# The last 64 features of q and k as one 128-column group in two token halves, q/k weights issued from ScalarE's queue, and a new operation order, in a fused attention and MLP kernel

## Chip, core and metric

The kernel runs on one core of one Trainium2 chip, as one program. The metric is device microseconds of one execution. All times are from the profile page, from the trace or from the timed runs.

## What is computed

Input `x` is 2048 tokens by 448 features in bf16. Two blocks follow each other, each behind a layer norm of its own and each added to its input:

```python
def _A_ref(x, wqkv, wo):                      # D = 448, H = 16 heads, Dh = 28
    W, dil = 8, 2
    qkv = (x @ wqkv).reshape(B, S, 3, H, Dh)...
    idx = pos[:, None] - arange(W)[None, :] * dil     # 8 keys, 2 tokens apart
    logits = einsum("bhsd,bhswd->bhsw", q, kg) * Dh ** -0.5
    attn = softmax(where(idx >= 0, logits, -1e9))
    o = einsum("bhsw,bhswd->bhsd", attn, vg)
    return o.reshape(B, S, D) @ wo

def _B_ref(x, w1, w2, w3, w4):                # F = 1792
    h = gelu(layernorm(x) @ w1)
    # four groups of 112 features, shifted by +1, -1, +2, -2 tokens
    hs = concatenate([g0, g1, g2, g3]) @ w2
    x1 = x + hs
    return x1 + gelu(layernorm(x1) @ w3) @ w4

h  = x + _A_ref(layernorm(x), wqkv, wo)
h2 = h + _B_ref(layernorm(h), w1, w2, w3, w4)
```

## The kernel before

The tokens are worked on in four blocks of 512 (t = 0 to 3) for attention and the first part of the MLP, and in five units of 2, 4, 4, 4 and 2 tiles of 128 tokens for the rest. A phase has a letter and the number of its block: N1 (norm), A1 (transpose, then q and k), V (values), A2 (products of q with the eight shifted keys, and their sums over heads), S (softmax), A3 (attention times values), O (output projection), B1 and M (second norm, `w1`, gelu), B2 and T (`w2`, third norm), W3 (`w3`, gelu), B3 (`w4`, store).

The program records all operations first (`_Sched.group`, reached through `mms`, `steps`, `act`, `dve`, `pool` and `dma`), each with what it depends on. `ORDER` is a list of operation numbers: `_Sched.arrange` gives each engine its operations in that order, hands out the buffers (eight PSUM banks, `actT`, `lntm` and others) in that order, and derives the waits. Every engine's queue and SyncE's DMA queue (SP) is therefore a fixed list. `OTHER` names the operations that go to a second engine that could also do them. Since all instructions are emitted by one line, the profile gives the line L1010 for nearly all of them; they are told apart by tile names.

The contraction over 448 features is cut into chunks at 0, 128, 192 and 320, so that each matmul uses 64 rows: `duo` runs two sums side by side, one on partitions 0 to 63 and one on 64 to 127, and swaps them for the second half, which waits for the first (`sdeps`). A pair of such matmuls is written "64*128" in the profile: 64 rows, 128 columns of the array.

Features 0 to 383 of q and of k are three groups of 128 columns each. The last 64 features of q and of k are a fourth group (the lines from `X, Y = _Tile(P_bank), _Tile(P_bank)` on in `phase_A1`). There the array is cut into 64 by 64 pieces ("64*64" in the profile), 28 matmuls for each block of tokens. Even pieces of 64 tokens land on partitions 0 to 63 and odd ones on 64 to 127. Then `X` (q) is copied to `qT` with one copy, `Y` (k) to `kr` with one copy, and two or three small copies fill the 16 columns ahead of each piece of `kr`, from which the shifted keys of A2 are read.

At the start `WARM` matmuls of 512 columns on the identity keep TensorE busy (`keep_busy`); `FILL` can put more between the first transposes. SP issues all loads: tiles 0, 1, and 2 with 3 of `x`, the q/k weights in two halves (`load_rows`, "arena<-in_A_wqkv_dram", 448 KB each), tiles 4 to 7, the v weights, the rest. Every matmul of q and k needs both halves of the q/k weights.

Of the kernel before, what the change touches and what calls it, by code (L numbers as in the profile page):

```python
# [50 lines left out]
"""  # L51
OTHER = """
92 182 483 489 492 495 546 552
"""
FULL = (4,)
FILL = (0, 0, 0, 0)
WARM = 11
FIRST = ((0, 1), (1, 1), (2, 2))


class _Pool:


# [219 lines left out]
def bass_sequential_preLN__sliding_local_dilated__mixer_s_mlp__prompt_kernel(  # L283
# [9 lines left out]
    PADK = 16  # L293
# [20 lines left out]
    with ExitStack() as es:  # L314
# [60 lines left out]
        def shifted(t, c):  # L375
            return bass.AP(AR, A_KV + t * KVB + c * KVW + PADK, [[A_END, 128], [64, 8] if c < 3 else [KW, 4], [-DIL, NW], [1, 64]])
# [675 lines left out]
```

## Time and profile before

| | |
|---|---|
| median of three timed runs | 189.51 us (188.73 to 191.31) |
| span of the profiled execution, first to last instruction | 186.4 us |
| time of the profiled execution | not on its page; the median lies 3.1 us above the span |
| TensorE matmul (PE) busy | 180.3 us, 97% of the span, 2496 matmuls |
| TensorE weight load (PEld) busy | 94.0 us, 50% |
| VectorE (DVE) busy | 127.0 us, 68%, 225 instructions |
| ScalarE (ACT) busy | 122.1 us, 65%, 289 instructions |
| GpSimd (POOL) busy | 24.0 us, 13%, 59 instructions |
| DMA | 18.59 MB, 41.5% of 16 engines' span on the program's queue |

A row of the timeline has the start, the time from the first start to the last end, engine, line, operation, the tiles written and read, rows and columns of the array for TensorE, shape and count; in brackets the idle time before and what ended it. A row of groups has the busy time, the mean ns of one, and the idle time before.

### The profile page before, as it was taken

To read this page: it belongs to the slowest core of one execution; us is meant where nothing else is said; L and a number is where in the kernel's file an instruction comes from. 1 tells how busy PE (TensorE), PEld (TensorE's weight loads), DVE (VectorE), ACT (ScalarE), POOL (GpSimd) and SP (SyncE) were. 2 spreads that over 40 slices of the span, in tenths; PEclk is the share of its full clock that TensorE was granted. 3 is DMA by queue.
4 is the path that set the end of the run, shared out by engine and by line. 5 is a ranking of instruction groups with operands and counts; after the bars stand their busy time and mean duration, and the time that the engine had idled before them with its cause. 6 is when DMAs were issued, how large, how long until landed. Compare 5 with 4: busy or idle time off the path is not lost.

```text
span 186.4 us, 5772 instructions
## 1 busy us (share of the span) xinstructions
PE 180.3 (97%) x2496; PEld 94.0 (50%) x2496; DVE 127.0 (68%) x225; ACT 122.1 (65%) x289; POOL 24.0 (13%) x59
## 2 busy tenths in 40 slices
PE   6899998999999999999999999999999999999994
PEld 2474333445544565765455544554445544555663
DVE  6799999999999999999476587614087274000403
ACT  3549999898999999957959489503833004730340
POOL 4320000000000000425300000170002805000000
PEclk9999999999999999999999999999999999999999
DMA  5999025865515667914360201491111602300121
GB/s 134 356 282 182 16 51 130 198 216 71 144 38 110 115 216 165 307 53 45 73 116 10 58 8 26 88 141 54 29 40 41 116 0 52 106 0 4 49 98 49
DMA packets 33633, 18.59 MB, mean 100 GB/s; under 512 B 21208, under 2 KB 33096, under 8 KB 33608
## 3 DMA queue, kind: packets, MB, share of 16 engines
q1 hardware_dynamic: 33608, 18.23, 41.5%
q8 instruction: 19, 0.31, 0.6%
q14 instruction: 6, 0.05, 0.1%
HBM read 8.14 MB, written 1.84 MB: 54 GB/s over the span
## 4 chain that ended last, share of the span: by engine, by line
PE 79%; DVE 14%; ACT 4%; DMA 1%; issue 0%; SPq 0%
PE ps L1010 79%; DVE qk_r L1010 9%; DVE st L1010 1%; ACT lntm L1010 1%; DMA xin<-in_A_x_dram 1%; DVE lntm L1010 1%; ACT L1010 1%; DVE mx L1010 1%; DVE xin L1010 1%; ACT arena L1010 1%; ACT h3T L1010 1%; DVE pb L1010 0%; DVE ls L1010 0%; DVE mv L1010 0%; ACT rs_x L1010 0%
## 5 line engine op out<-in xcount | busy, mean ns | idle before, releaser
L1010 PE MATMUL ps<-actT,arena 64*128 64x512 bf16 (+2 forms) x812 | 69.8, 326 | 0.9 <-DMA actT<-lntm 0.5
L1010 ACT ACTIVATE h3T<-ps 128x512 bf16<-128x512 f32 (+1 forms) x70 | 30.9, 517 | 38.5 <-PE ps L1010 38.4
L1010 PEld LDWEIGHTS ps<-actT,arena 64*128 64x128 bf16 (+1 forms) x812 | 35.4, 96 | 31.9 <-PE ps L1010 1.9
L1010 PE MATMUL ps<-arena,h3T 64*128 64x448 bf16 (+3 forms) x434 | 44.9, 343 | 0.2
L1010 ACT ACTIVATE arena<-ps 128x512 bf16<-128x512 f32 (+6 forms) x66 | 30.7, 508 | 8.5 <-PE ps L1010 8.1
L1010 PEld LDWEIGHTS ps<-arena,h3T 64*128 64x128 bf16 (+1 forms) x434 | 22.6, 94 | 20.0 <-ACT h3T L1010 0.6
L1010 DVE TENSOR_TENSOR qk_r<-arena 128x4096 bf16<-128x4096 bf16 (+1 forms) x16 | 31.9, 2013 | 0.1
L1010 DVE SCALAR_TENSOR_TENSOR qk_r<-ps,mrs,arena 128x448 bf16<-128x448 f32 (+2 forms) x17 | 10.4, 651 | 30.9 <-PE ps L1010 30.9
L1010 POOL TENSOR_TENSOR arena<-arena,xin 128x448 f32<-128x448 f32 x16 | 16.1, 1035 | 77.9 <-ACT lntm L1010 65.5
L1010 DVE TENSOR_TENSOR bd_r<-arena,bmask 80x2048 bf16<-80x2048 bf16 x16 | 19.0, 1214 | 1.7 <-PE ps L1010 1.7
L1010 DVE SCALAR_TENSOR_TENSOR arena<-xin,rs_y,ps 128x448 f32<-128x448 bf16 x16 | 10.3, 671 | 11.0 <-PE ps L1010 11.0
L1010 PE MATMUL ps<-wo_s,actT 64*128 64x448 bf16 x128 | 14.5, 350 | 0.1
L1010 PE MATMUL ps<-actT,w_s 64*112 64x512 bf16 x112 | 13.4, 379 | 0.0
L1010 PE MATMUL ps<-w_s,arena 64*128 64x448 bf16 x83 | 12.8, 349 | 0.1
L1010 PE MATMUL ps<-arena,actT 64*128 64x448 bf16 x112 | 12.3, 351 | 0.2
L1010 ACT ACTIVATE actT<-ps 128x512 bf16<-128x512 f32 (+2 forms) x19 | 11.7, 639 | 1.1 <-PE ps L1010 1.0
L1010 ACT ACTIVATE lntm<-xin,nm 128x448 bf16<-128x448 bf16 x16 | 10.6, 672 | 1.1 <-DVE nm L1010 1.1
L1010 DVE BATCH_NORM_STATS2 st<-xin 128x6 f32<-128x448 bf16 x16 | 9.2, 614 | 1.0 <-DMA xin<-in_A_x_dram 0.9
L1010 PEld LDWEIGHTS ps<-actT,w_s 64*112 64x112 bf16 x112 | 7.2, 126 | 4.4 <-ACT arena L1010 0.3
L1010 ACT ACTIVATE rs_x<-mv,epsilon 128x4 f32<-128x4 f32 (+2 forms) x16 | 4.6, 298 | 6.4 <-DVE mv L1010 6.3
L1010 PEld LDWEIGHTS ps<-w_s,arena 64*128 64x128 bf16 x83 | 5.5, 95 | 6.1 <-PE ps L1010 0.5
L1010 ACT ACTIVATE vt<-ps 128x448 bf16<-128x448 f32 x16 | 8.3, 546 | 0.5 <-PE ps L1010 0.5
(73 smaller groups left out, 161.6 us busy)
## 6 DMA issues: line engine op xcount, KB each, us to landing
arena<-in_B_w_dram SPq DMA_DIRECT2D x2, 896.0 KB, 5.9
out_dram<-qk_r SPq DMA_DIRECT2D x15, 112.0 KB, 1.8
arena<-in_B_w_dram SPq DMA_DIRECT2D x2, 784.0 KB, 7.3
vw<-vt SPq DMA_DIRECT2D x4, 320.0 KB, 4.3
vw<-vt SPq DMA_DIRECT2D x4, 256.0 KB, 4.1
arena<-in_A_wqkv_dram SPq DMA_DIRECT2D x2, 448.0 KB, 4.7
xin<-in_A_x_dram SPq DMA_DIRECT2D x2, 448.0 KB, 7.5
xin<-in_A_x_dram SPq DMA_DIRECT2D x3, 224.0 KB, 5.5
```

The costliest lines, as they stand in the source:

```text
L1010: inst = getattr(eng, meth)(**kw)
```

## The change

1. In `phase_A1` the last 64 features of q and of k become one group of 128 columns. Their weights are first copied side by side into a new tile `wl` (`setup_last`, one copy on GpSimd behind the q/k weights' arrival). The 512 tokens are two halves of 256, which are the two sums of one `duo`: 14 matmuls of 64 rows, 128 columns and 256 tokens. Of each half, partitions 0 to 63 of the bank hold q and 64 to 127 hold k. Two copies go to `qT`, two to `kr`, one small copy fills the columns ahead of the second half and, but for the last block, one those of the next block.
2. `kr` is now one row of 16 + 256 columns for each half. `phase_A2`, the end of S and `phase_A3` address tokens in the new arrangement, with the same shapes of work.
3. Both halves of the q/k weights are issued by ScalarE. The load of tiles 4 and 5 now waits for the landing of tiles 2 and 3.
4. `ORDER` and `OTHER` are new, `WARM` goes from 11 to 7, and one filler matmul stands between the first transposes.

```diff
 ORDER = """
-8 9 2 10 12 0 1 39 40 41 42 43 44 45 46 47 48 49 13 5 14 4 15 16 6 33 7 50 17 18 29 51 36 37 34 30 52 55 53 54 56 62
+0 1 5 40 41 8 9 10 7 33 29 30 11 14 32 15 31 47 42 52 48 2 49 50 12 53 54 57 59 58 16 17 34 35 55 60 61 62 18 19
...
 OTHER = """
-92 182 483 489 492 495 546 552
+183 184 482 485 491 497 554
 """
-FILL = (0, 0, 0, 0)
-WARM = 11
+FILL = (1, 0, 0, 0)
+WARM = 7
...
-        kr = [arv(A_KV + t * KVB + 3 * KVW, 128, 4 * KW).rearrange("p (j n) -> p j n", j=4) for t in range(NST)]
+        kr = [arv(A_KV + t * KVB + 3 * KVW, 128, PADK + 256) for t in range(NST)]
...
-        load_x(2, 2)
+        first = load_x(2, 2)
+        load_rows("wqk", wqkv_s[:, :, 0:2 * D], A_wqkv, 0, 2 * D, "act")
         act(zs[:, 0, 0:1], epsilon[:, 0:1], ACT.Exp)
-        load_rows("wqk", wqkv_s[:, :, 0:2 * D], A_wqkv, 0, 2 * D)
-        load_x(4, 2)
+        load_x(4, 2, after=[first])
...
+        def setup_last():
+            pool("tensor_copy", out=wl[:].rearrange("p c (g n) -> p c g n", g=2),
+                 in_=wqkv_s[:, :, D - 64:3 * D - 64].rearrange("p c (g n) -> p c g n", g=2)[:, :, :, 0:64])
...
-            X, Y = _Tile(P_bank), _Tile(P_bank)
...
-            copy(qT[:, 3, now:now + 256], X(lambda v: v[:, 0:256]))
-            copy(kr[t][:, :, PADK:], Y(lambda v: v[:, 0:256].rearrange("p (j n) -> p j n", j=4)), False)
-            copy(kr[t][64:128, :, 0:PADK], last(0, 0, 4), False)
-            copy(kr[t][0:64, 1:4, 0:PADK], last(0, 1, 3), False)
+            ends = []
+
+            def half(h):
+                b = _Tile(P_bank)
+                ends.append(b)
+                return sums(lambda lo, n: b(lambda v: v[:, 0:256].rearrange("p (i n) -> p i n", i=2)),
+                            lambda c, part: wl[part, c, :],
+                            lambda c, part, lo, n: rows(a, c, 2 * h, 2, part), h == 0)
+
+            duo(half(0), half(1), ((0, 256),))
+            for h, b in enumerate(ends):
+                copy(qT[64 * h:64 * h + 64, 3, now:now + 256], b(lambda v: v[0:64, 0:256]))
+                copy(kr[t][64 * h:64 * h + 64, PADK:], b(lambda v: v[64:128, 0:256]), False)
+            copy(kr[t][64:128, 0:PADK], ends[0](lambda v: v[64:128, 256 - PADK:256]), False)
             if t + 1 < NST:
-                copy(kr[t + 1][0:64, 0:1, 0:PADK], last(3, 1, 1), False)
+                copy(kr[t + 1][0:64, 0:PADK], ends[1](lambda v: v[64:128, 256 - PADK:256]), False)
```

The start of TensorE's queue, before; "ident" alone is a warm-up matmul, "ident,lntm" a transpose, "actT,arena" a matmul of q or k of block 0, and its 64x256 form the last 64 features:

```order
L1010 MATMUL ps<-ident 128x512 x11
L1010 MATMUL ps<-ident,lntm 128x128 x16
L1010 MATMUL ps<-actT,arena 128x256 x66
L1010 MATMUL ps<-actT,arena 64x256 x16
L1010 MATMUL ps<-actT,arena 128x256 x6
L1010 MATMUL ps<-actT,arena 64x256 x12
L1010 MATMUL ps<-actT,arena 128x256 x6
```

The same place now, where "actT,wl" is the new group of block 0 and the third row the filler:

```order
L1008 MATMUL ps<-ident 128x512 x7
L1008 MATMUL ps<-ident,lntm 128x128 x4
L1008 MATMUL ps<-ident 128x512
L1008 MATMUL ps<-ident,lntm 128x128 x12
L1008 MATMUL ps<-actT,arena 128x256 x52
L1008 MATMUL ps<-ident,lntm 128x64 x32
L1008 MATMUL ps<-actT,arena 128x256 x20
L1008 MATMUL ps<-actT,wl 128x256 x8
L1008 MATMUL ps<-actT,arena 128x256 x12
L1008 MATMUL ps<-actT,wl 128x256 x6
```

Four warm-up matmuls are gone, the 28 small matmuls are 14 wide ones of the same form as their neighbours, and each of the two halves of the group has other work behind it.

The start of ScalarE's queue, before; "rs_x" and "rs_y" are the two steps from a variance to its inverse root, for tile 0, tile 1, tiles 2 and 3, and then tiles 4 to 7, "actT" the copies of the transposes, "arena<-ps" those of q and k:

```order
L1005 ACT_TABLE_LOAD
L1010 ACTIVATE rs_x<-mv,epsilon 128x1
L1010 ACTIVATE rs_y<-rs_x 128x1
L1010 ACTIVATE rs_x<-mv,epsilon 128x1
L1010 ACTIVATE rs_y<-rs_x 128x1
L1010 ACTIVATE rs_x<-mv,epsilon 128x2
L1010 ACTIVATE rs_y<-rs_x 128x2
L1010 ACTIVATE actT<-ps 128x512 x3
L1010 ACTIVATE mx<-epsilon 128x1
L1010 ACTIVATE rs_x<-mv,epsilon 128x4
L1010 ACTIVATE rs_y<-rs_x 128x4
L1010 ACTIVATE arena<-ps 128x512 x4
```

The same place now:

```order
L1008 DMA arena<-in_A_wqkv_dram 128x2x896
L1003 ACT_TABLE_LOAD
L1008 ACTIVATE rs_x<-mv,epsilon 128x1
L1008 ACTIVATE rs_y<-rs_x 128x1
L1008 DMA arena<-in_A_wqkv_dram 128x2x896
L1008 ACTIVATE rs_x<-mv,epsilon 128x1
L1008 ACTIVATE rs_y<-rs_x 128x1
L1008 ACTIVATE rs_x<-mv,epsilon 128x2
L1008 ACTIVATE rs_y<-rs_x 128x2
L1008 ACTIVATE actT<-ps 128x512 x4
L1008 ACTIVATE rs_x<-mv,epsilon 128x4
L1008 ACTIVATE rs_y<-rs_x 128x4
```

The first half of the weights stands first, the second half behind the inverse root of tile 0, and a fourth copy of transposes, which VectorE did before, has come in.

VectorE's queue from the first normalizations to the first product of A2, before ("BN_STATS" and "BN_AGGR" make a tile's mean and variance, "lntm" is its normalization, "COPY" that fourth copy, "bmask" a constant, "qk_r" the product; ahead of these rows the "BN_AGGR" of tile 0 stood right behind its "BN_STATS"):

```order
L1010 BN_AGGR mv<-st 128x2
L1010 TENSOR_SCALAR lntm<-xin,mv,rs_y 128x448
L1010 BN_AGGR mv<-st 128x2
L1010 TENSOR_REDUCE bmask<-ls 80x4x8
L1010 TENSOR_SCALAR lntm<-xin,mv,rs_y 128x448 x2
L1010 COPY actT<-ps 128x512
L1010 BN_STATS st<-xin 128x6 x4
L1010 BN_AGGR mv<-st 128x2 x4
L1010 TENSOR_REDUCE bmask<-ls 80x4x8
L1010 TENSOR_SCALAR lntm<-xin,mv,rs_y 128x448 x4
L1010 BN_STATS st<-xin 128x6 x2
L1010 TENSOR_TENSOR qk_r<-arena 128x4096
```

And now:

```order
L1008 TENSOR_REDUCE bmask<-ls 80x4x8 x2
L1008 BN_STATS st<-xin 128x6 x2
L1008 BN_AGGR mv<-st 128x2 x2
L1008 BN_STATS st<-xin 128x6 x2
L1008 BN_AGGR mv<-st 128x2 x2
L1008 TENSOR_SCALAR lntm<-xin,mv,rs_y 128x448 x4
L1008 BN_STATS st<-xin 128x6 x4
L1008 BN_AGGR mv<-st 128x2 x4
L1008 MEMSET pb 128x320
L1008 TENSOR_SCALAR lntm<-xin,mv,rs_y 128x448 x4
L1008 BN_STATS st<-xin 128x6 x4
L1008 TENSOR_TENSOR qk_r<-arena 128x4096
```

The variance of tile 0 now stands behind the statistics of tile 1, all statistics of tiles 0 to 3 ahead of the first normalization, and those of tiles 8 to 11 all ahead of the first product instead of two of the four.

More of the change, by code (lines that the diff above doesn't have):

```diff
@@ L635, in setup_late @@
             late("memset", ap=kk[0][:, :, 0:PADK], constant=0.0)
-            late("memset", ap=kr[0][0:64, 0, 0:PADK], constant=0.0)
+            late("memset", ap=kr[0][0:64, 0:PADK], constant=0.0)
             late("memset", ap=vw[0:PADK, 0, 0, :], constant=0.0)
@@ L691, in phase_A1 @@
                 ev_b()
-            X, Y = _Tile(P_bank), _Tile(P_bank)
-            both = ((X, D - 64, ((0, 1, 2, 3), (0, 2, 3))), (Y, 2 * D - 64, ((0, 1, 3), (0, 1, 2, 3))))
-            op = None
-            for second in range(2):
-                turned = [op] * second
-                specs = []
-                (bu, wu, cu), (bl, wl, cl) = both[::-1] if second else both
-                for n, (ct, cb) in enumerate(zip(cu[0], cl[1])):
-                    for e in range(2):
-                        for b, w, c, part in ((bu, wu, ct, TOP), (bl, wl, cb, BOT)):
-                            specs.append((e, dict(out=b(lambda v, e=e: v[64 * e:64 * e + 64, 0:256].rearrange("p (i n) -> p i n", i=4)),
-                                                  lhsT=wqkv_s[part, c, w:w + 64], rhs=a(lambda v, e=e, c=c, part=part: v[part, :, c, 64 * e:64 * e + 64]),
-                                                  start=not second and n == 0, stop=bool(second) and n == 2), 256))
-                op = S.group("pe", [("matmul", kw) for _, kw, _ in specs], pe=[(n, "s", None) for _, _, n in specs])
-                op.sdeps.update(turned)
@@ L783, in turn @@
                 part = (TOP, BOT)[h]
-                return (h, dict(out=banks[h](lambda v: v[0:KW, 64 * r:64 * r + 64]), lhsT=pb[part, sl, r * KW:(r + 1) * KW], rhs=ident[part, part],
+                return (h, dict(out=banks[h](lambda v: v[0:KW, 64 * r:64 * r + 64].rearrange("p (e j n) -> p j e n", e=2, j=2)), lhsT=pb[part, sl, r * KW:(r + 1) * KW], rhs=ident[part, part],
                                 start=True, stop=True), 64)
@@ L788, in phase_A2 @@
             for h, b in enumerate(banks):
-                copy(pt[t].rearrange("p (n r) -> p n r", r=NW)[:, 64 * h:64 * h + 64, :], b(lambda v: v[0:KW, :].rearrange("p (r n) -> p n r", r=NW)))
+                copy(pt[t].rearrange("p (e h n r) -> p e h n r", e=2, h=2, r=NW)[:, :, h, :, :], b(lambda v: v[0:KW, :].rearrange("p (r e n) -> p e n r", r=NW, e=2)))
         def phase_A3(t):
@@ L797, in phase_A3 @@
                 dve("tensor_tensor", block=True, out=bd(lambda v: v.rearrange("p (n g r) -> p n g r", g=8, r=NW)),
[L798 to L799 removed]
+                    in0=bass.AP(pt[t].tensor, pt[t].offset + 32 * il * NW, [list(pt[t].ap[0]), [NW, 32], [0, 8], [1, NW]]),
+                    in1=bass.AP(bmask, 0, [[64, KW], [0, 32], [NW, 8], [1, NW]]), op=ALU.mult)
                 mms([(b(lambda v, j=j, lo=128 * c + 64 * a2: v[32 * j:32 * j + 32, lo:lo + 64]),
```

18 lines of the change are left out of this document (8 added, 10 removed), and 59 rows, old and new, of the table ORDER.

## Prediction

> **What bounds the kernel now.** First the busy times, the chain, and the busy time by stage:
>
> ```profile
> PE 180.3 (97%) x2496; PEld 94.0 (50%) x2496; DVE 127.0 (68%) x225; ACT 122.1 (65%) x289; POOL 24.0 (13%) x59
> PE 79%; DVE 14%; ACT 4%; DMA 1%; issue 0%; SPq 0%
> 12.00:35.00 23.00, 22.13 (x309) 9.60 (x308) 22.90 (x30) 21.89 (x59) 0.00 (x0) 1.00 0.57 110
> 35.00:80.00 45.00, 44.73 (x874) 23.74 (x876) 44.81 (x62) 43.49 (x107) 2.03 (x2) 1.00 0.64 158
> 80.00:117.00 37.00, 36.66 (x532) 19.03 (x530) 27.25 (x61) 28.20 (x61) 5.59 (x9) 1.00 0.25 47
> 117.00:184.00 67.00, 66.97 (x704) 36.14 (x698) 22.54 (x47) 23.36 (x51) 11.94 (x13) 1.00 0.25 57
> ```
>
> The columns of the last four rows are PE, PEld, DVE and ACT busy. TensorE is the bound: the chain runs through it for 79%, and from 117 us on it idles 0.03 us of 67. Up to 80 us, though, VectorE (22.90 of 23, 44.81 of 45) and ScalarE (21.89 and 43.49) are full as well. So a microsecond off TensorE's queue counts whole behind 80 us, and ahead of it only as far as the two others keep up. TensorE's own idle time there is small: 0.87 us in 12 to 35 and 0.27 in 35 to 80.
>
> The head is another matter, since there TensorE waits for data:
>
> ```profile
> 1.63 4.61 PE L1010 MATMUL ps<-ident 128*128 128x512 bf16 x11 [1.63 <-POOL mhalf L1010]
> 6.30 0.62 PE L1010 MATMUL ps<-ident,lntm 128*128 128x128 bf16 x8
> 7.39 0.70 PE L1010 MATMUL ps<-ident,lntm 128*128 128x128 bf16 x8 [0.47 <-DVE lntm L1010]
> 8.13 0.61 PE ps L1010 x8
> 8.78 4.35 PE ps L1010 x80
> 0.81 1.35 SPq L1010 DMA_DIRECT2D xin<-in_A_x_dram  x3
> 2.20 0.98 SPq L1010 DMA_DIRECT2D arena<-in_A_wqkv_dram  x2
> arena<-in_A_wqkv_dram SPq DMA_DIRECT2D x1, 448.0 KB, 4.1
> arena<-in_A_wqkv_dram SPq DMA_DIRECT2D x2, 448.0 KB, 4.7
> ```
>
> The real work starts at 8.13, with the first matmul of q. The first half of the weights is issued at 2.20 and lands 4.1 us later, at 6.3. The median of the two is 4.7, so the second took 5.3, and it was issued half of 0.98 us behind the first, at 2.7: it lands at 8.0. So that start hangs on the second weight half as much as on the transposes.
>
> **The change, part by part.**
>
> *The last 64 features.* One block's 28 small matmuls, what follows them, and a row of the wide form:
>
> ```profile
> 43.46 1.23 PE L1010 MATMUL ps<-actT,arena 64*64 64x256 bf16 x28
> 44.61 0.42 PE L1010 MATMUL ps<-bd_r,vw 80*32 80x64 bf16 x32
> ...
> 14.07 0.49 PE L1010 MATMUL ps<-actT,arena 64*128 64x256 bf16 x6
> 14.40 0.22 PE L1010 MATMUL ps<-ident,lntm 64*128 64x64 bf16 x4
> ```
>
> From start to next start the 28 take 44.61 − 43.46 = 1.15 us. The wide form stands below: six matmuls, that is three pairs, in 14.40 − 14.07 = 0.33, 0.11 us a pair. Fourteen are 7 pairs, 0.77 us. That is 0.38 a block and **−1.5 us** for four. The small form doesn't stream more columns: seven rounds of four against seven pairs, both of 256. So what I count on is the rest of the 1.15: the wait of the second half for the first, by the program, now filled with other work, and whatever lies between two tile shapes. Bounds: nothing, if both remain, and some 2 us, if the change into the small form costs a tenth of a microsecond too, ahead of its first row where I can't see it. I take 1.5, the nearest rows. Half of it falls ahead of 35 us, where VectorE sets the pace, half behind.
>
> [...]
>
> *The copies.* ScalarE's groups for the old copies:
>
> ```profile
> L1010 ACT ACTIVATE arena<-ps 128x256 bf16<-128x256 f32 x8 | 2.9, 392 | 0.0
> L1010 ACT ACTIVATE arena<-ps 64x64 bf16<-64x64 f32 x4 | 0.9, 216 | 0.1
> L1010 ACT ACTIVATE arena<-ps 64x48 bf16<-64x48 f32 x4 | 0.8, 208 | 0.1
> L1010 ACT ACTIVATE arena<-ps 64x16 bf16<-64x16 f32 x3 | 0.5, 181 | 0.1
> ```
>
> Before, 5.1 us. Now sixteen copies of 256 columns over half the partitions and seven small ones. A copy's time here goes by its columns: 128 by 256 takes 2.9/8 = 0.36, and I price 64 by 256 at the same (from below, the 0.22 of 64 by 64). That is 16 × 0.36 + 7 × 0.17 = 7.0 us, 1.9 more, all before 80 us. ScalarE's idle time in 12 to 80 is 1.11 + 1.51 = 2.6 us, which hides it; what it costs when that cover is gone is the second rival.
>
> *The copy of weights* on GpSimd waits for the second weight half. Its price lies between the 0.2 us of a small copy and the 1.0 of a 128x448 sum there:
>
> ```profile
> L1010 POOL COPY zc<-ls 128x48 bf16<-128x48 bf16 (+1 forms) x3 | 0.6, 213 | 0.1
> L1010 POOL TENSOR_TENSOR arena<-arena,xin 128x448 f32<-128x448 f32 x16 | 16.1, 1035 | 77.9 <-ACT lntm L1010 65.5
> ```
>
> Behind it in GpSimd's queue stand the memset of the key padding, which the first product of A2 needs, and the mask. With the weights at 9.3 (below) even the dear copy is done by 10.5, well ahead of any product. Cost nothing.
>
> *The head.* Rows for VectorE and ScalarE:
>
> ```profile
> 2.88 0.63 DVE L1010 BATCH_NORM_STATS2 st<-xin 128x6 f32<-128x448 bf16 x1 [0.40 <-DMA xin<-in_A_x_dram]
> 3.83 0.63 DVE L1010 BATCH_NORM_STATS2 st<-xin 128x6 f32<-128x448 bf16 x1
> 3.54 0.18 DVE L1010 BATCH_NORM_AGGREGATE mv<-st 128x2 f32<-128x6 f32 x1
> 3.76 0.29 ACT L1010 ACTIVATE rs_x<-mv,epsilon 128x1 f32<-128x1 f32 x1 [1.67 <-DVE mv L1010]
> 4.08 0.20 ACT L1010 ACTIVATE rs_y<-rs_x 128x1 f32<-128x1 f32 x1
> xin<-in_A_x_dram SPq DMA_DIRECT2D x1, 224.0 KB, 2.9
> 8.71 1.15 DVE L1010 BATCH_NORM_STATS2 st<-xin 128x6 f32<-128x448 bf16 x2 [0.46 <-DMA xin<-in_A_x_dram]
> 11.11 0.38 DVE L1010 TENSOR_REDUCE bmask<-ls 80x32 bf16<-80x256 bf16 x1
> 11.67 1.07 ACT L1010 ACTIVATE arena<-ps 128x512 bf16<-128x512 f32 x2
> 14.28 2.29 DVE L1010 TENSOR_TENSOR qk_r<-arena 128x4096 bf16<-128x4096 bf16 x1
> ```
>
> The first weight half is issued at once by ScalarE, 1.4 us earlier. The second stands behind the inverse root of tile 0, which now waits for the statistics of tile 1: 3.83 + 0.63, then 0.18, then from 3.76 to 4.28 on ScalarE, so it goes out at about 5.2 instead of 2.7. Its landing then takes 4.1 us by the nearest row (the first half, which also had 448 KB of x beside it): 9.3. Ends: 5.3 us, the old second half, gives 10.5; no queue at all, about 3.4 (2.9 for 224 KB and some 0.5 for as much again), gives 8.6. So the real work starts 1.2 us late, between 0.5 and 2.4. Before, its first eight matmuls took 0.65 us to 8.78, where four pairs need 0.44; that 0.2 is gone when all transposes are there, which leaves **+1.0 us**. The four warm-up matmuls and the filler lie in the wait and count nothing.
>
> Tiles 4 and 5 now wait for the landing of tiles 2 and 3, at 1.73 + 2.9 = 4.6, and everything queued on SP behind them (tiles 6 and 7, v weights, later tiles, `wo`) goes with them. But the 896 KB of weights no longer stand ahead. I take them in at about 8.2, between 7.5 (another 2.9 us) and 9.3, instead of 8.7. VectorE waited 0.46 us for them, and it also loses a bmask (0.38) from the stretch from 8.71 to 14.28 and the copy to ScalarE. At 14.28 it still owed two statistics of 0.57, which now stand ahead. I put it 0.7 us ahead at the same point of its work, though its first product may start no earlier. This matters because ScalarE's first copies of q and k stood at 11.67 behind an inverse root that waited for those statistics, not for TensorE. So the late weights don't delay VectorE, and about half of TensorE's 0.87 us idle in 12 to 35 goes: **−0.4**.
>
> *The rest of the order* I cost at nothing: changes of tile shape other than those of the small form stay as they are but for two more, and VectorE gives the S3 multiplication to GpSimd behind 80 us, where 37 − 27.25 of VectorE's time is idle.
>
> **Sum.** −1.5 + 1.0 − 0.4 = −0.9, against the span of 186.4: 185.5. The median lies 3.1 us above the span, so about **188.6 us**. Its own bounds: start +0.3 to +2.2, features 0 to −2, idle time 0 to −0.87; with one of the three at its end that is 187.9 (start) at best and 190.1 (features) at worst.
>
> **Rivals.**
>
> *Cold clock (slower).* Eleven warm-up matmuls of 512 columns took 4.61 us, 0.42 each, while TensorE at full rate takes 0.21 for 448:
>
> ```profile
> L1010 PE MATMUL ps<-arena,h3T 128*128 128x448 bf16 x14 | 3.0, 353 | 0.0
> ```
>
> So all of them ran at half rate, and the first transposes (eight of 128 columns in 0.62) no longer did. Full rate came after some 4.6 us of unbroken work; the granted clock in the windows shows 1.00 throughout and can't tell. Seven take 2.9 us and end near 4.6, and then TensorE has little until 9.3. If that isn't enough, the first 4.6 us of real work run at half rate and lose 2.3 us: 190.9. It decides if the first pairs stand 0.22 apart instead of 0.11. Against it: the transposes and the filler in between may suffice, since nothing here shows how much work holds the clock. [...]
>
> *ScalarE takes the gain.* It gets 1.9 us more against 2.6 of idle time, and what idles for TensorE's results can't all be filled. If it falls behind by the 0.9, the time is unchanged, 189.5.
>
> *Faster.* The weights land by 8.6 (+0.3), all the idle time goes (−0.87), and the features give 2: −2.6, 186.9 (186.4 − 2.6 + 3.1).
>
> *The group doesn't do what it says.* If the second half still waits for the first, only the change of shape goes, perhaps 0.1 a block: 189.6.
>
> **How the numbers follow.** Forecast 0.42 (its range 187.9 to 190.1), cold clock 0.25, ScalarE 0.15, faster 0.14, group without effect 0.04. The range reaches from 185.9, a microsecond below the faster case, to 191.6, most of the cold clock with its weights late. About 2% is what a measurement of this kernel can tell from no change: under 185.7 I put 0.08 (the faster case and a microsecond that I have not seen), over 193.3 0.05 (cold clock, weights at 10.5 and features at nothing together), 0.87 between.
>
> **What would show it.** Fourteen "actT,wl" matmuls in about 0.77 us, four times, and none of 64*64. The second weight half issued near 5.2 and landing near 9.3; the first q matmul just behind it, pairs 0.11 apart. VectorE's first product near 14.3 with all four statistics before it. ScalarE's 64x256 copies at 0.36. Most likely wrong: the landing, whose contention between two queues no run shows, and the clock.

## The result, and the profile after

The changed kernel takes **197.92 us** (median of four runs, 196.83 to 199.47) against 190.41 for the one before on the same chip (188.73 to 192.32): ratio **1.043**, 95% interval 1.035 to 1.051. The forecast was 188.6 with a range of 185.9 to 191.6, so the result lies 6 us outside it, on the other side of no change. In the tables below the medians are of all runs, while the ratios and intervals leave out runs more than 1.5% above the fastest of the same kernel.

The busy times, the granted clock over 40 slices of the span, and the chain, from the page of the changed kernel (profiled execution 199.47 us, the slowest of the four; span 197.8):

```profile
PE 182.7 (92%) x2437; PEld 96.9 (49%) x2437; DVE 128.3 (65%) x222; ACT 128.7 (65%) x297; POOL 26.2 (13%) x61
PEclk9759999999999999999969999999999999999999
PE 57%; ACT 16%; DMA 12%; DVE 9%; SPq 2%; issue 2%; POOL 1%; ACTq 0%
```

TensorE is busy 2.4 us longer with 59 matmuls fewer; the clock row has two dips, slices 2 and 3 and slice 21, and at the first of them 52 matmuls took 5.01 us from 10.50 on, 0.19 us a pair instead of 0.11. TensorE's share of the chain falls from 79% to 57%, and ScalarE and DMA, 5% together before, now hold 28%. The waits of TensorE (what it waited for, total us, times, longest):

```profile
PE ps L1008 <- DVE lntm L1008: 2.8, 1, 2.8
PE ps L1008 <- DMA actT<-lntm: 2.3, 2, 2.0
PE ps L1008 <- issue: 1.4, 2, 0.9
PE ps L1008 <- ACT arena L1008: 1.1, 2, 0.7
PE ps L1008 <- DMA ht<-arena: 1.0, 2, 0.6
```

The same stages as in the prediction, with the same columns:

```profile
12.00:35.00 23.00, 21.68 (x278) 11.73 (x276) 20.64 (x31) 20.02 (x54) 0.89 (x6) 0.94 0.59 144
35.00:80.00 45.00, 43.63 (x780) 22.20 (x782) 43.23 (x54) 42.94 (x109) 0.00 (x0) 1.00 0.60 140
80.00:117.00 37.00, 34.05 (x558) 19.50 (x554) 24.37 (x50) 26.67 (x58) 8.50 (x11) 0.95 0.30 56
117.00:184.00 67.00, 65.41 (x670) 32.26 (x669) 27.70 (x61) 30.52 (x57) 12.42 (x14) 1.00 0.23 46
```

TensorE's idle time grew in every stage: 0.87 to 1.32, 0.27 to 1.37, 0.34 to 2.95, and 0.03 to 1.59 us in the last. With 0.94 and 0.95 in the clock column, two stages ran partly at half rate besides (0.50 in the windows further below). Of the 5.7 us of new idle time, 4.2 stand behind 80 us, where the prediction put the new order at nothing.

### The profile page after: what moved, and what is told of

It is laid out like the page before. It is cut to its first block, busy times and chain, and to the rows that moved or that the text cites. A ratio compares the mean times of both kernels' runs of the same rounds, so it can differ in the third digit from the quotient of the medians.

```text
span 197.8 us, 5662 instructions
## 1 busy us (share of the span) xinstructions
PE 182.7 (92%) x2437; PEld 96.9 (49%) x2437; DVE 128.3 (65%) x222; ACT 128.7 (65%) x297; POOL 26.2 (13%) x61
## 4 chain that ended last, share of the span: by engine, by line
PE 57%; ACT 16%; DMA 12%; DVE 9%; SPq 2%; issue 2%; POOL 1%; ACTq 0%
PE ps L1008 57%; ACT arena L1008 7%; DMA actT<-lntm 5%; DMA vw<-vt 3%; ACT lntm L1008 3%; DVE st L1008 2%; SPq L1008 2%; ACT actT L1008 2%; ACT vt L1008 2%; DVE lntm L1008 2%; DMA ht<-arena 2%; DMA xin<-in_A_x_dram 2%; DVE arena L1008 1%; DVE qk_r L1008 1%; ACT xin L1008 1%
## 5 line engine op out<-in xcount | busy, mean ns | idle before, releaser
L1008 PE MATMUL ps<-actT,arena 64*128 64x512 bf16 (+1 forms) x700 | 70.2, 347 | 4.3 <-DMA actT<-lntm 2.0
L1008 PEld LDWEIGHTS ps<-actT,arena 64*128 64x128 bf16 x700 | 35.4, 98 | 33.2 <-ACT arena L1008 2.5
L1008 PE MATMUL ps<-arena,h3T 64*128 64x448 bf16 (+3 forms) x434 | 44.4, 343 | 0.0
L1008 ACT ACTIVATE arena<-ps 128x512 bf16<-128x512 f32 (+4 forms) x70 | 32.3, 507 | 7.9 <-PE ps L1008 7.3
L1008 ACT ACTIVATE actT<-ps 128x512 bf16<-128x512 f32 (+2 forms) x21 | 13.0, 648 | 2.1 <-PE ps L1008 2.1
L1008 PE MATMUL ps<-arena,actT 64*128 64x448 bf16 x112 | 12.8, 350 | 0.1
L1008 DVE TENSOR_SCALAR lntm<-arena,mv,rs_y 128x512 bf16<-128x512 f32 x14 | 9.1, 705 | 3.7 <-POOL rs_y L1008 3.1
```

Source lines behind the costliest of these rows:

```text
L1008: inst = getattr(eng, meth)(**kw)
```

## The experiments

Ratios are to the kernel before, run beside each on the same chip. "Old" and "new" order are those of the kernel before and of the changed one, the operations that only one kernel has being put where their counterparts stand.

| run | what it is | median us | ratio, 95% interval |
|---|---|---|---|
| e1 | before, wide group alone | 192.15 | 1.0139 (1.0082 to 1.0196) |
| e2 | before, loads on ScalarE's queue alone | 192.55 | 1.0174 (1.0111 to 1.0237) |
| e3 | changed, loads back on SP | 194.49 | 1.0269 (1.0211 to 1.0327) |
| e4 | new order alone | 193.38 | 1.0208 (1.0165 to 1.0250) |
| e5 | e3 with 11 warm-up matmuls | 195.03 | 1.0242 (1.0165 to 1.0320) |
| e6 | changed, with 16 warm-up matmuls | 194.56 | 1.0210 (1.0158 to 1.0261) |
| e7 | e1 with fewer copies | 190.94 | 1.0046 (1.0011 to 1.0080) |
| e8 | before with copies split | 192.68 | 1.0134 (1.0060 to 1.0208) |
| e9 | before with fewer matmuls | 189.45 | 0.9986 (0.9961 to 1.0011) |
| e10 | e6, late part in old order | 192.80 | 1.0164 (1.0118 to 1.0209) |
| e11 | before, ScalarE relieved by POOL | 189.54 | 0.9984 (0.9958 to 1.0009) |
| e12 | e2 with 16 warm-up matmuls | 190.58 | 1.0052 (1.0013 to 1.0090) |
| e13 | before, VectorE relieved | 190.40 | 0.9981 (0.9937 to 1.0025) |
| e14 | e1, VectorE relieved | 192.31 | 1.0099 (1.0072 to 1.0127) |
| e15 | e1, ScalarE relieved by POOL | 191.66 | 1.0070 (1.0031 to 1.0108) |
| e16, e18 | e4 with 16 warm-up matmuls, twice | 197.43, 196.91 | 1.0336 (1.0255 to 1.0417), 1.0360 (1.0317 to 1.0403) |
| e17 | before, all three relieved | 189.28 | 0.9983 (0.9945 to 1.0020) |

### The parts one by one (e1 to e4)

The wide group alone, in the kernel before (the new code of `phase_A1`, `wl` and the new addressing of `kr`; order, loads and warm-up are those of before):

```diff
-            X, Y = _Tile(P_bank), _Tile(P_bank)
...
+            duo(half(0), half(1), ((0, 256),))
```

> The kernel before with the wide group alone: the 128-column pass, the wl copy on POOL and the copies that go with it, in the order of before, loads on SP's queue, 11 warm-up matmuls. By the prediction's first step it gains 1.5 us (190.4 to 188.9, 0.4 us per block). The rival that ScalarE's seven more copies take the gain back (+1.9 us of copies) gives 190.4 or a little above. If the group itself were what made the change slow, it would come near 197.9.

The loads alone, in the kernel before:

```diff
-        load_rows("wqk", wqkv_s[:, :, 0:2 * D], A_wqkv, 0, 2 * D)
-        load_x(4, 2)
+        load_rows("wqk", wqkv_s[:, :, 0:2 * D], A_wqkv, 0, 2 * D, "act")
+        load_x(4, 2, after=[first])
```

> The kernel before with the loads of the q/k weights alone moved to ScalarE's queue (second half behind the first Exp of tile 0, tiles 4 and 5 behind the landing of tiles 2 and 3), everything else of before. Theory 'head': the second half lands 2 us later and TensorE starts its real work later, +1.5 to +2.5 us, so 192 to 193; with a clock that drops as well, up to 195. Theory 'order': the loads cost little, the loss comes with the new order, so 190.4 to 191.0.

The same lines turned back in the changed kernel (the load of tiles 4 and 5 too):

```diff
-        load_rows("wqk", wqkv_s[:, :, 0:2 * D], A_wqkv, 0, 2 * D, "act")
+        load_rows("wqk", wqkv_s[:, :, 0:2 * D], A_wqkv, 0, 2 * D)
```

> The changed kernel with the loads of the q/k weights put back on SP's queue, right behind tiles 2 and 3, new order and wide group kept, 7 warm-up matmuls. TensorE's lag behind its own work stood at 9.9 us at 19 us in the changed kernel and at 5.3 us at 13 us in the one before. Theory 'head': the loads and the clock that they cost explain the whole loss, so about 190 (197.9 less 7 or more). Theory 'order': only the 4.5 us of the head come back, 193 to 194, and the rest stays between 19 and 145 us.

The new `ORDER` and `OTHER` in the kernel before, and with them:

```diff
-FILL = (0, 0, 0, 0)
-WARM = 11
+FILL = (1, 0, 0, 0)
+WARM = 7
```

> The new order alone: the old group of small matmuls and the loads on SP's queue as before, but the order, the operations given to other engines and the 7 warm-up matmuls of the changed kernel. Theory 'order': 190.4 plus the 8.5 us that the changed kernel loses between 19 and 145 us less what the group would save, 195 to 199. Theory 'head': near before, 190 to 192.

No part gains. Group 1.4%, loads 1.7%, order 2.1%; neither theory had the group on the losing side. Putting the loads back gives 1.6% of the 4.3% back; e3's 194.5 us lie near what "order" said (193 to 194) and far from "head" (about 190). e4's 193.4 lie between the two theories. What each loses by is tested next.

### The clock (e5, e6, e12, e16, e18)

The windows of the changed kernel, cut at the times where the granted clock changes and at 3.41 us from these (columns as above, the clock third from the end):

```profile
0.99:4.40 3.41, 2.81 (x7) 0.89 (x7) 2.39 (x5) 1.28 (x1) 1.33 (x9) 1.00 0.69 194
4.40:7.81 3.41, 0.61 (x6) 0.34 (x6) 2.79 (x10) 1.49 (x6) 0.00 (x0) 1.00 0.53 151
7.81:11.23 3.42, 2.42 (x22) 1.79 (x22) 2.22 (x5) 2.17 (x4) 2.04 (x14) 0.50 1.03 346
96.56:99.97 3.41, 1.41 (x30) 0.90 (x26) 2.38 (x4) 2.73 (x9) 2.71 (x4) 1.00 0.52 116
99.97:103.38 3.41, 3.41 (x20) 1.51 (x18) 2.86 (x6) 2.44 (x5) 0.00 (x0) 0.50 0.13 24
```

The seven warm-up matmuls fill 2.81 us of a window and the clock is granted at 4.40. In the next TensorE works 0.61 us, since the first transposes come at 7.45, and two windows at a clock of 0.50 follow; the clock is back at 14.64. Likewise from 96.56 on, where the wait of 2.0 us for a transposing DMA leaves 1.41 us of work: one window at 0.50 follows, to 103.38. All edges in this trace (4.40, 7.81, 14.64, 99.97 and 103.38 us) are one or several times 3.41 us apart, and the window ahead of the second loss holds 1.41 us of work, against 0.61 ahead of the first.

e6 adds warm-up matmuls until the transposes come, and e12 does so in e2:

```diff
-WARM = 7
+WARM = 16
```

> The changed kernel with 16 warm-up matmuls instead of 7, nothing else. In it the clock was granted at 4.40 us and lost again from 7.82 to 14.64, after TensorE had stood idle from 4.65 to 7.45. Theory 'clock': with the gap filled the clock stays and 2.3 to 3.3 us come back, a ratio of 1.025 to 1.031 to the kernel before instead of 1.043. Rival: TensorE waits for the late tiles and weights whatever its clock is, and the time stays near 1.043.

> As e2 (the loads of the q/k weights moved to ScalarE's queue, all else as before; 192.55, ratio 1.017), but with 16 warm-up matmuls instead of 11. In e2 the clock was lost from 8.03 to 11.44 us and from 48.98 to 52.40. Theory 'clock': the loads cost only by the gap that they open before the first transposes; with it filled the time is 190 to 191. Rival 'lateness': the weights and tiles land later and TensorE starts later, clock or not: 192 to 192.7.

The clock row of e6 and then the one of e2:

```profile
PEclk9999999999999999999999999999999999999999
```

```profile
PEclk9889999999699999999999999999999999999999
```

Both came out on the side of "clock": 1.043 to 1.021, intervals apart, 4.1 us where 2.3 to 3.3 were expected, and 1.0174 to 1.0052, within the expectation. The loads cost 1.0 us in themselves and the rest by the gap that they open. Not all of the 4.1 us can be put down to the warm-up: at half rate TensorE lost, as an estimate, 2.9 us in the head of the profiled execution and 1.7 at 100 us (half of its 5.8 and 3.4 us of work at a clock of 0.50 there), and e6 has the same late wait (1.9 us) in a window with 1.56 us of work that kept the clock. Counted back from the edges in steps of 3.41 us, the first window begins at 0.99 us in the changed kernel and at 0.73 in e4. Of the changed kernel's four runs two show a mean granted clock of 1.00 at 196.8 and 198.4 us; that does not speak against it, since the column shows 1.00 ahead of the first grant too (0.99 to 4.40 above, where five warm-up matmuls take 2.11 us, 0.42 each, twice the 0.21 behind the grant in e5), and e4 shows 1.00 throughout although its first real matmuls took 4.19 us, where 26 pairs at 0.11 would take 2.9:

```profile
8.51 4.19 PE L1010 MATMUL ps<-actT,arena 64*128 64x256 bf16 x52
```

Where the loads are on SP, longer warm-up did not pay. e5 has 11 matmuls:

```diff
-WARM = 7
+WARM = 11
```

> The changed kernel with the q/k weights' loads on SP's queue, as in e3, and 11 warm-up matmuls instead of 7. In e3 the clock was granted only at 9.73 us, in e4 at 10.97; in the kernel before, at 5.83. Theory 'clock': the seven matmuls (1.59 to 4.55 us) are too few, TensorE's first real matmuls ran at half rate; with eleven the clock is there at 6 us and 2.0 to 2.5 us come back, 192.0 to 192.5 against e3's 194.5. Rival: what the head loses is the order of its work and not the clock; then it stays at 194 to 195.

It did not come: 1.0269 to 1.0242, within the intervals. TensorE's lag (the time less the matmul work at full rate done by then) is 1.2 us smaller at 13 us than in e3, and at the end of the kernel it is 0.5 us larger: the transposes behind the first 52 matmuls start 0.36 us earlier with four warm-up matmuls more done (0.21 us each), and the span ends 1.3 us later. And e16, 16 matmuls in e4, went the wrong way:

> e4 (the new order alone, old group, loads on SP's queue, ratio 1.0208) with 16 warm-up matmuls instead of 7, so that the clock is there before the first real matmuls. Theory 'clock': most of the order's loss was the cold clock up to 10.97 us, 1.003 to 1.010 remains for its late waits (e10 gave 0.9 us back by these). Rival: the order itself loses 3 us and more in its middle, 1.015 to 1.022.

> The kernel of e16 once more (the new order alone with 16 warm-up matmuls, ratio 1.034), for a second profile: in the first one the clock was lost from 22.08 to 28.91 us after TensorE had waited 2.0 us at 19.62. If that loss is what made e16 slower than e4 (1.021), a run without it should show a span of 191 to 192. If the span is 194 to 196 with the clock kept all along, the cause is a longer wait somewhere else, to be read from its rows.

The profile of e18 has the clock from 7.13 us on and no loss, and a span of 194.6. The rows of its TensorE, and of e4's:

```profile
18.51 1.06 PE L1010 MATMUL ps<-actT,arena 64*64 64x256 bf16 x15
21.69 1.69 PE L1010 MATMUL ps<-actT,arena 64*128 64x512 bf16 x11 [2.12 <-issue]
```

```profile
19.16 1.71 PE L1010 MATMUL ps<-actT,arena 64*128 64x512 bf16 x12
21.74 0.39 PE L1010 MATMUL ps<-actT,arena 64*128 64x512 bf16 x2 [0.87 <-issue]
```

Both resume at 21.7, after a wait that nothing in the profile releases, and in e4, e16 and e18 alike it stands behind TensorE's matmul number 222, whatever that computes (e16 and e18 have nine more warm-up matmuls ahead; in e16 the wait is 1.70 us, from 20.00 on). The traces have transfers of 16 KB each on a queue of the kind "instruction" (19 of them, 0.31 MB, before, in the changed kernel and in e18); the first one ran here:

```
before 14.36 to 15.75    e4 19.04 to 20.15    e16 19.12 to 20.23    e18 18.82 to 20.08
```

Counted with TensorE's weight loads and the few others of its queue, 449 instructions lie ahead of the wait at 21.7. The traces have more waits that nothing releases: behind instruction 1217 in e2 (1.65 us), behind 1473 in the changed kernel (0.48), e1, e3, e5, e6 and others, behind 2241 in the changed kernel (0.95), e3 and e5. From 449 these are 3, 4 and 7 times 256 further on. The one behind 449 ended 1.4 to 1.6 us after the first of the transfers was through, the others 1.2 to 1.6 us after the fourth, the fifth and the eighth. The places of the waits and the ends of these transfers thus go together, in steps of 256 instructions; that the one waits for the other is not shown beyond these times. Such waits take 1.4 us in the changed kernel (its row "issue" above), none before. So whatever the head of e16 and e18 gains is lost at 21.7.

Why the first transfer is late in the new order was not tried. One load stands out: the first half of `w3` (896 KB), issued at 11.43 us in e4 and at 35.58 before; the DMA engines' busy share from 14 to 20 us is 1.07 in e4 and 0.80 before. The wait explains 1.25 of the 2.9 us that lie between e18 and e4 by their ratios. The rest stands at 69.8 us, where e18 waits 1.65 us for ScalarE and e4 does not; why ScalarE is late there remains open.

### The group: copies against matmuls (e7, e8, e9)

ScalarE's copies of the group in the changed kernel, and the wide matmuls of block 3, 0.77 us from start to next start (0.44 for the eight, 0.33 for the six):

```profile
L1008 ACT ACTIVATE arena<-ps 64x256 bf16<-64x256 f32 x16 | 6.0, 375 | 0.3
L1008 ACT ACTIVATE arena<-ps 64x16 bf16<-64x16 f32 x7 | 1.2, 174 | 0.1
53.58 0.61 PE L1008 MATMUL ps<-actT,wl 64*128 64x256 bf16 x8
54.78 0.49 PE L1008 MATMUL ps<-actT,wl 64*128 64x256 bf16 x6
```

Both prices are close to those of the prediction, 7.2 us of copies (7.0) and 0.11 a pair.

In e1 the matmuls do not come so cheap. There the two halves stand right behind each other, and the fourteen took 1.0, 1.2 and 1.2 us in blocks 1 to 3; this is block 2:

```profile
44.81 1.18 PE L1007 MATMUL ps<-actT,wl 64*128 64x256 bf16 x14
46.01 0.42 PE L1007 MATMUL ps<-bd_r,vw 80*32 80x64 bf16 x32
```

Over the four blocks TensorE saved 0.4 us in e1 and 1.3 in the changed kernel. So the gain on TensorE hangs on the new order, which puts other work between the halves, and e1 prices the group's copies nearly alone.

e8 adds such copies to the kernel before and nothing else, e7 takes them from e1:

```diff
-            copy(qT[:, 3, now:now + 256], X(lambda v: v[:, 0:256]))
+            S.group("act", [("activation", dict(out=qT[64 * h:64 * h + 64, 3, now:now + 256], in_=X(lambda v, h=h: v[64 * h:64 * h + 64, 0:256]), func=ACT.Copy)) for h in range(2)])
```

> The kernel before, with the two 128x256 copies of each block's last features split into two copies of 64 partitions each: eight copies more on ScalarE, 16 x 0.376 less 8 x 0.392 = 2.9 us of its time more, TensorE's work unchanged. Theory 'ScalarE': that time is not hidden, +2 to +3 us, 192 to 193. Rival 'hidden' (the prediction's third step): ScalarE's idle time takes it, 189.7 to 190.3.

```diff
+                if h == 0:
+                    copy(qT[:, 3, now:now + 256], b(lambda v: v[:, 0:256]))
+                    copy(kr[t][:, PADK:], b(lambda v: v[:, 0:256]), False)
+                else:
+                    copy(qT[64:128, 3, now:now + 16], b(lambda v: v[0:64, 0:16]))
+                    copy(kr[t][64:128, PADK:PADK + 16], b(lambda v: v[64:128, 0:16]), False)
```

> As e1 (the wide group alone in the order of before), but ScalarE's copies are cut: the first half's two copies take all 128 partitions, those of the second half only 16 of 256 columns, so half of the last features of q and k are left wrong. ScalarE's copies of the group fall from 7.3 us to about 5.8, near the 5.4 us of before, TensorE's work is that of e1. Theory 'ScalarE': e1 lost because ScalarE, full from 14 to 80 us, got 1.9 us more; without them 188.7 to 190. Rival 'group': the wide group loses on TensorE itself (its waits for the weights or the order that it forces), and the time stays at 192.

2.9 us of copies cost 2.5 us (1.1 to 4.0 by the interval), and 1.5 us of them taken away give 1.8 back. e7 is a little above its expectation. TensorE's waits from 12 us on in the kernel before (its only row), e1 and e8 (the first three of each) name the engine:

```profile
PE ps L1010 <- DMA actT<-lntm: 0.5, 1, 0.5
```

```profile
PE ps L1007 <- ACT arena L1007: 1.4, 2, 0.8
PE ps L1007 <- DMA actT<-lntm: 1.0, 2, 0.5
PE ps L1007 <- ACT vt L1007: 0.8, 1, 0.8
```

```profile
PE ps L1011 <- ACT arena L1011: 1.1, 3, 0.6
PE ps L1011 <- ACT vt L1011: 1.1, 1, 1.1
PE ps L1011 <- DMA vw<-vt: 0.8, 1, 0.8
```

e9 turns to the other side, the matmuls:

```diff
                 for n, (ct, cb) in enumerate(zip(cu[0], cl[1])):
+                    if n != (2 if second else 0):
+                        continue
```

> The kernel before with 20 of the 28 small matmuls of each block's last features left out (q's and k's last 64 features are then wrong): TensorE's work falls by 4 x 20/28 x 1.15 = 3.3 us, which is more than the wide group could ever save, and nothing else changes. Theory 'full engines': between 8 and 86 us VectorE is busy 76.8 of 78 us and ScalarE 70.2, so less work for TensorE shortens the span by 1.2 us at most: 189.0 to 190.2. Rival 'TensorE is the bound' (the prediction's first step): 3.3 us, 187 or below.

Its relief was smaller than written: the eight small matmuls of a block took 0.5 to 0.9 us, for the wait of the second half for the first remains, so TensorE got 1.9 us less, not 3.3. Of these 0.25 us arrived (at most 0.74 by the interval). Where the rest went, in e9 and then before:

```profile
28.22 0.62 PE L1012 MATMUL ps<-qk_r,zc 128*32 128x512 bf16 x8
29.94 1.25 PE L1012 MATMUL ps<-actT,arena 64*128 64x512 bf16 x10 [1.10 <-DMA actT<-lntm]
```

```profile
28.86 0.61 PE L1010 MATMUL ps<-qk_r,zc 128*32 128x512 bf16 x8
29.97 1.25 PE L1010 MATMUL ps<-actT,arena 64*128 64x512 bf16 x10 [0.49 <-DMA actT<-lntm]
```

TensorE arrives 0.64 us earlier and goes on at the same time, when the transposed tiles of block 2 land. What it gained ahead of this landing is gone there. Another 0.6 us go at a second landing of this kind at 66.4, and 0.7 to a wait that nothing releases, behind instruction 1473; before has neither.

### Which engine sets the pace up to 80 us (e11, e13, e14, e15, e17)

e11 gives work of ScalarE to POOL, e13 halves six of VectorE's products, e14 and e15 do the same in e1, e17 has all three reliefs:

```diff
-                copy(kk[t + 1][:, :, 0:PADK], kk[t][:, :, 512:KVW])
+                pool("tensor_copy", out=kk[t + 1][:, :, 0:PADK], in_=kk[t][:, :, 512:KVW])
...
-            norms = norms_of("B1", t, 4)
+            norms = norms_of("B1", t, 4) if t else "appa"
```

> The kernel before with ScalarE relieved: the three 128x48 copies of the keys' edges (245 ns) and two normalizations of the block-0 MLP input (820 ns) go to POOL, which is idle there; ScalarE has 2.4 us less, nothing is left out. By e8's price (2.5 us for 2.9 us of copies) up to 2 us less; since VectorE has only 1.2 us idle between 8 and 86 us, theory 'full engines' gives 0.5 to 1.2 us: 189.0 to 189.7. Rival: POOL is slower than ScalarE at this and what waits for it comes late, or POOL slows VectorE: 190.5 to 192.

> e1 (the wide group alone, 1.0139) with 2.4 us of ScalarE's work on POOL as in e11, all of the result computed. e7, with 1.4 us of ScalarE's copies less, stood at 1.0046. Theory 'ScalarE': 1.000 to 1.006, the wide group is then no loss, and no gain either, since TensorE's time is worth little (e9). Rival: where the copies stand, right behind the group, matters and not their sum; 1.010 to 1.014.

```diff
+                n = 2 if c == 3 and t else wide
...
+                m = 16 if il == 3 and t else 32
```

> The kernel before with VectorE relieved: in blocks 1 to 3 half of the last q*k product and half of the fourth product with the mask are left out (six instructions of 1214 ns halved, about 3.6 us; the result is then wrong there). TensorE 3.3 us lighter gave 0.25 us (e9), ScalarE 2.4 us lighter gave 0.16 (e11). Theory 'VectorE sets the pace': 2.5 to 3.5 us less, 186.2 to 187.2. Theory 'all three at once': the next full engine takes over, 0 to 1.5 us less, 188.2 to 189.7.

> e1 (the wide group alone, ratio 1.0139) with the same VectorE work left out as in e13. If the group's loss is ScalarE's time alone, it stays with VectorE relieved: about 2.5 us above e13. If it comes from VectorE being kept waiting at the worst places, e13's relief takes it away and the two come within 1 us of each other.

> The kernel before with the three reliefs of e9, e11 and e13 together: TensorE 3.3 us lighter (20 of 28 small matmuls per block left out), ScalarE 2.4 us lighter (to POOL), VectorE 3.6 us lighter (six products halved; the result is wrong). Each alone gave 0.16 to 0.36 us. Theory 'all three at once': only together do they show, -2 to -3 us, 187 to 188 (0.984 to 0.990). Rival: the pace there is set by latencies between the engines, not by their work, and the sum is that of the three alone, about -0.8 us, 0.996.

Relief of one engine gives nothing that can be measured, and my theory that only all three together would show **falls with e17**: 0.3 us (1.0 at most by the interval), not 2 to 3, though the reliefs were smaller than written (1.9 us for TensorE, and 3.2 for VectorE, whose halved products took 0.68 us each). The pace up to 80 us is not the sum of any engine's work, full as all three look. TensorE's waits in e17 from 12 us on:

```profile
PE ps L1016 <- DMA ht<-arena: 1.1, 2, 0.8
PE ps L1016 <- DMA actT<-lntm: 1.1, 1, 1.1
```

2.2 us are waits for transfers, against 0.5 before: the gain ends at DMA landings, as in e9. POOL spoils the test in part, since its copies of 128x48 took 1.3 to 4.8 us where ScalarE took 0.25. As to the group, e14 is 2.2 us above e13, so its loss stays with VectorE relieved, and e15 gets half of it back with ScalarE relieved, in intervals that overlap. That speaks for ScalarE's time, and for where it falls as well; e15's 1.007 lies just above the band for the sum alone, and the two are not separated.

### The late part of the order (e10)

The chain of the changed kernel from 89 us on (start, us, what):

```profile
90.14 1.03 POOL rs_y L1008
...
91.20 2.62 DVE lntm L1008 x4
...
93.85 5.26 DMA actT<-lntm
...
99.25 4.87 PE ps L1008 x27
```

W3 of unit 1 waits for a transposition whose input VectorE finishes at 93.8. e10 puts the order of before, with the engines that it gives to these operations, from position 450 (about 80 us) on into e6:

```diff
 ORDER = """
...
-555 556 392 601 609 602 606 538 610 614 484 557 394 399 558 561 562 603 395 559
+539 540 544 543 541 475 609 601 555 610 556 602 558 557 561 562 611 560 563 392
...
```

> As e6 (the changed kernel with 16 warm-up matmuls, ratio 1.021), but from position 450 of the order on, about 80 us, the rest stands in the order of before. In e6 TensorE's lag grows from 15.1 us at 76 us to 20.2 at 140, in steps of 2.1 at 92 to 97, 1.2 at 114 to 119 and 0.9 at 135 to 140, where it waits for transposing DMAs and for ht; in the kernel before from 12.2 to 13.8. Theory 'order': with the late order of before these steps go, -3 to -3.5 us, ratio 1.002 to 1.006. Rival: they come from what is late earlier and stay, 1.015 to 1.021.

The waits behind 80 us, in e6 and in e10:

```profile
PE ps L1007 <- DMA actT<-lntm: 1.9, 1, 1.9
PE ps L1007 <- DMA ht<-arena: 1.2, 2, 0.7
```

```profile
PE ps L1007 <- ACT h3T L1007: 0.7, 1, 0.7
```

The waits go, and the profiled span falls by 2.3 us (193.2 to 190.9). The medians fall by less: 1.0210 to 1.0164, 0.9 us, and the intervals overlap. So the waits are the late order's, shown by the rows; that they cost 1 to 2 us is probable, and the 3 us that I expected did not come.

The pieces by ratios: loads 0.5% (e12), group 1.4% (e1), late order 0.5% (e6 to e10), clock 2.2% (to e6), together 4.6%, against 4.3% measured. They need not add: e3 and e4, which have the new order without the loads that came with it, are dearer than their shares here, the group is another on TensorE in e1 than in the changed kernel, and the 1.4 us of waits that nothing releases have no piece of their own. That the sum comes near is no proof of the pieces.

## Why the prediction was wrong, point by point

The sum said −0.9 us and the time rose by 7.5. Three steps of it failed. It carried TensorE's saving whole into the span, where e9 shows 0.25 us for 1.9. It put the copies at nothing as hidden in ScalarE's idle time, where e8 shows 2.5 us for 2.9. And it left the cold clock and the late part of the new order out of the sum, where e6 shows 4.1 us and e10 some 1 to 2.

- **Features, −1.5 us.** Fourteen wide matmuls took 0.77 us in three of the four blocks, and all four took 1.3 us less than before, close to what was worked out. What failed is the step from TensorE's time to the span. I had written that ahead of 80 us a microsecond counts only as far as the others keep up, and then entered the 1.5 in full. e9 shows 0.25 for 1.9. The rival "the group doesn't do what it says" (0.04) came true for most of the saving in e1, where the halves stand together, and not in the changed kernel. What a change of tile shape costs by itself no run shows: the 0.1 us a block of that rival equals the 0.4 us over four blocks in e1, but other things differ there too.
- **Copies, hidden in 2.6 us of idle time.** Size right (7.2 us for 7.0), cover wrong: 2.9 us of copies cost 2.5 (e8). Of the 2.6 us of ScalarE's idle time 1.8 were waits for TensorE's results, at places of their own; a copy that is due elsewhere is not hidden there. The rival "ScalarE takes the gain" had the mechanism, but stopped at no change (189.5); e1 passed it by 1.4%.
- **Head, +1.0 us.** Late tiles and weights were named, their size was not. The second half went out at 6.15, not 5.2, because tile 1's statistics began at 5.01 instead of 3.83: the x loads slowed with 448 KB beside them. With the loads alone it is the same (4.99 in e12), and in e3, with the loads back, tile 1 makes VectorE wait no more. The half was there when POOL copied it, and the first q matmul started at 10.50:

```profile
5.01 0.63 DVE L1008 BATCH_NORM_STATS2 st<-xin 128x6 f32<-128x448 bf16 x1 [1.11 <-DMA xin<-in_A_x_dram]
6.15 0.40 ACTq L1008 DMA_DIRECT2D arena<-in_A_wqkv_dram  x1
10.47 0.61 POOL L1008 COPY wl<-arena 128x512 bf16<-128x512 bf16 x1 [0.60 <-DMA arena<-in_A_wqkv_dram]
10.50 5.01 PE L1008 MATMUL ps<-actT,arena 64*128 64x256 bf16 x52 [1.00 <-ACT actT L1008]
10.17 1.68 DVE L1008 BATCH_NORM_STATS2 st<-xin 128x6 f32<-128x448 bf16 x3 [1.20 <-DMA xin<-in_A_x_dram]
16.31 2.29 DVE L1008 TENSOR_TENSOR qk_r<-arena 128x4096 bf16<-128x4096 bf16 x1 [0.15 <-ACT arena L1008]
```

  2.4 us late, the end of the bound and not its middle. The q row names ScalarE's copies as what ended the wait, but these were done at 10.21; the landing of the weights, which POOL's row names, came last.
- **−0.4 for VectorE ahead.** The reverse: three of the four statistics of tiles 4 to 7 waited 1.20 us for x until 10.17, and the first product came at 16.31 instead of 14.28.
- **The cold clock, a rival at 0.25 and 190.9.** What was to decide it was seen: 52 matmuls took 5.01 us, 0.19 a pair. It was priced as one cold stretch of 2.3 us. In fact the clock was granted, lost in a gap, and in the profiled execution lost again at 100 us; by e6 it comes to 4.1 us, the second loss in part. It was the largest single term and belonged in the forecast.
- **The rest of the order, nothing.** The late waits for transposing DMAs and `ht` are the step left out: 3.3 us of waiting in the profile, some 1 to 2 in the time (e10). The waits that nothing releases, 1.4 us, stood in no term either; what they cost in the time was not tried.
- **The bound on "slower", 0.05.** It needed the cases together, each put at its own chance. Late weights and the cold clock had a common cause, the gap ahead of the first data, and came together; the features came to nothing for a reason of their own (e9), and the cost of the late order was not in the bound at all.

## What to carry to other kernels

Before booking a microsecond taken off a full-looking engine, find the landing that it waits for next: in front of a transfer that landed no earlier the gain was worth nothing (e9: TensorE came 0.64 us earlier and went on at 29.94 instead of 29.97), while work added to ScalarE, which feeds TensorE, was paid almost in full (e8: 2.5 us for 2.9). The gap of 2.8 us in TensorE's work cost itself here and two windows at half clock behind it, and more warm-up work took 2.2% off in e6 and 1.2% in e12, so try it with a change that delays the first data; where the gap was shorter (1.4 us in e3, 1.5 in e4, ahead of the first transposes), more warm-up gave nothing (e5) or lost (e16). A new list of operations can lose by itself (e4, 2.1%): take the parts apart on the chip, and look at each part's own rows, since the same code cost TensorE 4.1 us in one order (e1) and 3.2 in another.

## What the runs showed of the hardware

The windows of 3.41 us ahead of a loss of the clock hold 0.61 and 1.41 us of TensorE's work in the changed kernel (above), 1.43 and 1.69 in e2 (the second below), 1.71 in e16 and even 1.92 in e13. A window of 1.71 us in e4 and one of 1.56 in e6 kept it. For the first grant 2.63 us were not enough in e5 (from 0.80 us on; the clock came at 7.63), 2.67 in e17 and 2.81 in the changed kernel were. The windows of e2, and the wait in the first of them:

```profile
45.57:48.98 3.41, 1.69 (x78) 1.02 (x64) 2.09 (x2) 1.83 (x7) 0.00 (x0) 1.00 0.40 78
48.98:52.40 3.42, 3.42 (x56) 1.46 (x50) 2.00 (x2) 1.84 (x5) 0.00 (x0) 0.50 0.97 84
47.33 0.21 PE L1010 MATMUL ps<-bd_r,vw 80*32 80x64 bf16 x3 [1.65 <-issue]
```

As an estimate from these windows alone, the edge lies near half a window for losing it (1.7 of 3.41 us) and near 0.78 of one for the first grant (2.65). It is not sharp, since windows that kept it lie below others that lost it, and in e16 a window with 3.36 us of work behind a loss (from 22.08 us on) did not bring it back; the ends of matmuls are modelled. With seven warm-up matmuls the clock came at 4.40 in the changed kernel, whose window from 0.99 on holds 2.81 us of work, and at 10.97 in e4, whose window from 0.73 on holds 2.55.

POOL's copy of 128x48 in bf16, 0.21 us in the setup, took 1.28, 1.65 and 5.39 us in the middle of e11, with VectorE busy beside it:

```profile
L1012 POOL COPY arena<-arena 128x48 bf16<-128x48 bf16 x3 | 8.3, 2773 | 28.1 <-ACT arena L1012 28.1
```

Each ended 0.08 us behind the end of a product on VectorE (at 16.94, 28.55 and 46.91 us), and in e17 the three end likewise behind 16.20, 27.82 and 45.37. That the copies waited for VectorE is my reading of these six ends, since a slow layout would not make them end there; which of VectorE's instructions would hold such a copy, no run separates.

And TensorE had waits that nothing in the profile releases, behind its instructions 449 (0.87 to 2.12 us in e4, e16 and e18), 1217 (1.65 in e2), 1473 (0.48 in the changed kernel) and 2241 (0.95 there). Each ended 1.2 to 1.6 us after a 16 KB transfer of the kind "instruction" was through, above. The loss of the clock in e2 at 48.98 follows such a wait.
